# Attention into a mixture of experts on one core: order of the first loads, and products of ones in the first softmax

## The chip, the cores and the metric

The kernel runs on one core of a Trainium2 chip. The time is the device time of one execution in microseconds (us); three executions of the kernel before are shown, and their median is compared with that of the changed kernel. The profile comes from one further execution of its own. The engines are TensorE (PE, with its weight loads PEld), VectorE (DVE), ScalarE (ACT), GpSimd (POOL) and SyncE (SP), which here only issues transfers.

## The reference

There are four batches of q, k and v with 5056 rows of 256 channels, and eight experts with 1024 hidden units. A batch's attention is over channels, so its matrix is only 256 by 256, but it is a sum over all rows:

```
qn = q / (norm(q, axis=1) + 1e-6);  kn = k / (norm(k, axis=1) + 1e-6)
a  = softmax(kn.T @ qn / tau)              # 256 x 256 for each batch
x  = (v @ a).reshape(20224, 256)           # one row for each token
expert = argmax(x @ w_gate);  g = softmax(x @ w_gate)[expert]
out    = g * (relu(x @ w1[expert]) @ w2[expert])
```

## The kernel before

Each batch has two passes. The first reads q and k in 20 chunks (L205), adds up the products kn.T @ qn on PE (L225, or L229 and L230 where a chunk is split in two parts) and the squares of the entries on ACT and DVE (L215 to L218). Then comes the softmax (L242 to L327): the sums of squares go through PE into the PSUM tile `ntp`, DVE works out the reciprocal norms, two products with a diagonal (L272) spread those of q over the other half of `ntp`, DVE copies that half out (L287) and scales (L292), ACT takes the exponential (L299), PE transposes (L310), DVE copies (L314), PE multiplies by the gate's weights (L318), and DVE puts the result beside the attention matrix as `a_x` (L322). The second pass goes over v in ten groups of 512 tokens, each in two half groups (two `yield`s): first half, load v, `px` on PE (L365), copies and squares on ACT (L370, L372); second half, scale (L378), 16-bit rows on ACT and DVE (L386, L387), the choice of the expert and each row's place on DVE and PE (L395 to L442), and four scatters into the DRAM table `xs` from POOL's queue (L445).

The experts' weights are loaded and split into two 16-bit parts on the chip, by the generator `weights()`: 32 loads of 512 KB (L120), four for an expert, and for each matrix 16 products on PE for a scale (`gram`, L158), a diagonal (`w_diag`, L162), a product (L123), the scale (L84, L85), and a split of 128x2048 entries on ACT (L112) and then DVE (L113). One step of it issues one load; the splits of an expert's two matrices come with the first and the third load of the expert behind it. The second matrices of the last two experts are loaded into the tag `hl`, of two buffers, which also holds the squares of the next batch's chunks (L213, L217).

Once the six first groups of batch 0 are in `xs`, `table(0)` gives the list of full blocks of 256 tokens, and `block()` loads one transposed (L586), copies its expert's weights (L604) and multiplies (L616, L638). From there on, blocks and the passes of the batches that follow are interleaved by the pacing at L741 to L755.

The order of the work around the change is that of the Python program: its instructions are taken in this order for each engine, and where one isn't ready by the framework's planning, a later one can go ahead. All loads are in SP's queue. The main loop takes one half group of batch 0, some steps of the weights, and one chunk of batch 1, in turn. Step 20 (`step == nch`) is the first softmax; steps 21 and 22 are the first group's halves, and so on up to the sixth group:

```python
weighed = 0
for step in range(2, nch + 1 + 2 * CUT):
    take(first, 1)
    weighed += take(wts, 0 if step < nch else min(14 if step == nch else 2, 4 * E + 1 - weighed))
    if step > nch + 2:
        take(second, 1)
```

In the texts the experts' weights are counted in the order of loading (the first, the second, ...), and the splits too.

Of the kernel before, what the change touches and what calls it, by code (L numbers as in the profile page):

```python
# [10 lines left out]
F32 = mybir.dt.float32  # L11
# [9 lines left out]
P = 128  # L21
B, N, C = 4, 5056, 256
NP = 5120
E, F = 8, 1024
# [39 lines left out]
def attention_then_experts(ctx, tc, qk, vT, wts_in, kc, out):  # L64
    nc = tc.nc
    sync, act, vec, pool, pe = nc.sync, nc.scalar, nc.vector, nc.gpsimd, nc.tensor
# [6 lines left out]
    ps_h = ctx.enter_context(tc.tile_pool(name="ps_h", bufs=3, space=bass.MemoryType.PSUM))  # L73
# [111 lines left out]
    def split(raw):  # L185
# [3 lines left out]
        vec.tensor_tensor(out=hl[:, 1], in0=raw, in1=hl[:, 0], op=ALU.subtract)  # L189
        return hl  # L190

    def attention(b, s_split, x_split, acc):


# [4 lines left out]
        nch = len(s_split)  # L199
        behind = []  # L200
        for ch in range(nch):

            tag, bufs = (("raw", RAW), ("rows", 3), ("xg", 2), ("raw", RAW), ("rows", 3))[ch % 5 if b == 0 else 0]
# [39 lines left out]
        tp = ps_t.tile([P, 512], F32, tag="tp", name="ntp")  # L243
# [25 lines left out]
        for c in range(2):  # L269
            dg = soft[:, 0, c * P : (c + 1) * P]  # L270
            vec.tensor_scalar(out=dg, in0=ident, scalar1=rn[:, c : c + 1], scalar2=None, op0=ALU.mult)
            pe.matmul(tp[:, C + c * P : C + (c + 1) * P], ones, dg, start=True, stop=True)  # L272
        rq = tp[:, C : 2 * C]


        if x_split:
# [30 lines left out]
        tp = ps_t.tile([P, 512], F32, tag="tp", name="atp")  # L307
        for c1 in range(2):
            for c2 in range(2):
                pe.transpose(  # L310
                    tp[:, c2 * C + c1 * P : c2 * C + (c1 + 1) * P], a_x[:, c1, c2 * P : (c2 + 1) * P], ident
                )
        aT = soft[:, 5:7, :]
        vec.tensor_copy(out=aT, in_=tp.rearrange("p (c n) -> p c n", c=2))  # L314
        tp = ps_t.tile([P, 512], F32, tag="tp", name="gtp")
        for c1 in range(2):
            for c2 in range(2):
                pe.matmul(  # L318
                    tp[:, c1 * E : (c1 + 1) * E], aT[:, c2, c1 * P : (c1 + 1) * P], wg[:, c2, :],
                    start=(c2 == 0), stop=(c2 == 1),  # L320
# [21 lines left out]
        for g in range(G):  # L342
# [12 lines left out]
            for t in range(T):  # L355
                if b > 0:
                    px = ps_a.tile([P, C + E], F32, tag="acc", name="px")
                else:
                    pool_, tag = ((ps_y, "y0"), (ps_h, "hp"), (ps_y, "y1"), (ps_h, "hp"))[t]
                    px = pool_.tile([P, C + E], F32, tag=tag, name="px")  # L360
                ts = slice(t * P, (t + 1) * P)
                n = 0
# [58 lines left out]
            tp = ps_t.tile([P, 512], F32, tag="tp", name="rtp")  # L421
# [3 lines left out]
            for t in range(shifts):  # L425
                pe.matmul(
                    tp[:, t * E : T * E], ones16, ex[:, 0 : T - t, :].rearrange("p t e -> p (t e)"),
                    start=False, stop=(t == shifts - 1),
# [14 lines left out]
            for t in range(T):  # L443
                n = 64 if last and t == T - 1 else P
# [220 lines left out]
    def take(gen, n):  # L665
        for _ in range(n):
            next(gen, None)
        return n

    nch = NP // P // 2  # L670
    normal = [(ps_a, "acc")] * 2
    wts = weights()
    first = attention(0, [False] * nch, False, [(ps_y, "y0"), (ps_y, "y1")])
    second = attention(1, [i == 0 or i >= NATIVE for i in range(nch)], True, normal)

    ones16 = one.tile([P, P], F16, name="ones16")
    vec.memset(ones16, 1.0)
    idle = ps_t.tile([P, 512], F32, tag="tp", name="idle")
    for _ in range(30):
        pe.matmul(idle[:, 0:P], ones16, ones16, start=True, stop=True)  # L680
    take(first, 2)


# [22 lines left out]
    weighed = 0  # L706
    for step in range(2, nch + 1 + 2 * CUT):
        take(first, 1)
        weighed += take(wts, 0 if step < nch else min(14 if step == nch else 2, 4 * E + 1 - weighed))
        if step > nch + 2:  # L710
            take(second, 1)
    tables = {0: table(0)}

    def streams():
        tables[1] = table(1)
        for b in range(1, B):
            yield from second if b == 1 else attention(b, [True] * nch, True, normal)
            tables[b + 1] = table(b + 1)
            if b == B - 1:
                tables[LAST] = table(LAST)  # L720
            yield 0
# [76 lines left out]
```

## Time and profile before

| | us |
|---|---|
| median of 3 executions | 1184.86 (1183.29 to 1185.75) |
| the profiled execution | 1188.32 |
| its span, first to last instruction | 1186.6 |
| PE busy | 1153.5 (97%) |
| DVE busy | 899.4 (76%) |
| ACT busy | 643.5 (54%) |
| POOL busy | 392.3 (33%) |

The profiled execution is 1.7 us longer than its span, which is what lies around the first and the last instruction. A timeline row is: start and length in us, engine, line, operation, out<-in, shape, count, and in brackets the engine's idle time before it and what ended it. Rows of equal instructions in a row are merged.

### The profile page before, as it was taken

The page shows a single profiled execution, that of the slowest core. Times are in us where ns is not written, and L with a number is a line of the kernel's source. Part 1 is how long each engine was busy: PE and PEld are TensorE (multiplying, and loading weights), DVE is VectorE, ACT ScalarE, POOL GpSimd, SP SyncE. Part 2 cuts the span into 40 slices and gives each one's busy share as a digit, 9 for nine tenths or more (in the row PEclk, how much of TensorE's full clock was granted, in tenths as well). Part 3 has the DMA queues.
Part 4 walks back from the last instruction along what each step waited for, and adds up shares of the span by engine and source line. Part 5 has one row for each costly group of instructions (what it writes and reads, how often), then busy time and mean ns, then how long its engine had stood idle before and what let it go on. Part 6 is the DMA issues. An engine that isn't in the chain of part 4 may idle for free.

```text
span 1186.6 us, 28182 instructions
## 1 busy us (share of the span) xinstructions
PE 1153.5 (97%) x10242; PEld 1024.9 (86%) x10242; DVE 899.4 (76%) x2384; ACT 643.5 (54%) x1362; POOL 392.3 (33%) x366
## 2 busy tenths in 40 slices
PE   9798899999999999999999999999999999999998
PEld 8677688899888889999888889999988888889897
DVE  6789988778887877777888777776875566656886
ACT  6399854877655536665565536666533223332232
POOL 0046761466511123544422212455421111112121
PEclk9989989999999999999999999999999999999999
DMA  9977765445555524444354434443242222111121
GB/s 340 408 277 254 208 177 134 135 122 145 139 145 120 130 81 101 118 115 119 97 152 127 131 91 93 131 95 82 70 109 50 50 55 55 46 51 38 40 52 35
DMA packets 147871, 145.93 MB, mean 123 GB/s; under 512 B 115980, under 2 KB 117393, under 8 KB 147728
## 3 DMA queue, kind: packets, MB, share of 16 engines
q1 hardware_dynamic: 132336, 102.48, 33.0%
q0 software_dynamic: 15392, 41.60, 9.8%
q8 instruction: 82, 1.34, 0.5%
q14 instruction: 61, 0.50, 0.1%
HBM read 80.03 MB, written 43.29 MB: 104 GB/s over the span
## 4 chain that ended last, share of the span: by engine, by line
PE 57%; issue 24%; DVE 7%; POOL 5%; ACT 3%; DMA 3%; SPq 1%; POOLq 0%; DVEq 0%; ACTq 0%
PE y L638 20%; PE hp L616 19%; PE px L368 7%; POOL out L653 4%; PE sp L225 4%; PE sp L229 3%; DMA raw<-in_qk 2%; PE sp L230 2%; DVE W L113 1%; ACT xjunk L372 1%; PE px L365 1%; DVE rows L387 1%; DVE hl L189 1%; ACT W L112 1%; ACT xg L370 1%
## 5 line engine op out<-in xcount | busy, mean ns | idle before, releaser
L616 PE MATMUL hp<-xT,wp 128*128 128x256 f16 (+1 forms) x4320 | 450.0, 262 | 1.6 <-DVE ht L624 1.1
L638 PE MATMUL y<-wp,ht 128*128 128x256 f16 x3888 | 447.7, 273 | 0.0
L616 PEld LDWEIGHTS <-wp 128*128 128x128 f16 x4320 | 383.1, 98 | 46.1 <-issue 3.4
L638 PEld LDWEIGHTS <-ht 128*128 128x128 f16 x3888 | 373.9, 98 | 53.3 <-issue 4.7
L653 POOL DMA_INDIRECT out<-o,mt x162 | 184.9, 1141 | 628.5 <-ACT o L651 595.2
L604 DVE COPY wp<-W 128x1024 f16 x720 | 297.8, 425 | 116.0 <-PE y L638 65.3
L623 ACT ACTIVATE ht<-hp 128x512 f16<-128x512 f32 x324 | 191.6, 593 | 157.1 <-PE hp L616 143.1
L624 DVE SCALAR_TENSOR_TENSOR ht<-hp,ht 128x512 f16<-128x512 f32 x324 | 219.6, 686 | 22.6 <-ACT ht L623 16.6
L445 POOL DMA_INDIRECT xs<-rows,r_si x160 | 189.5, 1184 | 122.7 <-issue 41.8
L651 ACT ACTIVATE o<-y,b_fac 128x256 f32<-128x256 f32 x162 | 68.8, 470 | 207.2 <-PE y L638 196.6
L368 PE MATMUL px<-a_h,hl 128*128 128x264 f32 x480 | 98.1, 296 | 0.0
L386 ACT ACTIVATE rows<-xg,x_sc 128x256 f16<-128x256 f32 x160 | 69.9, 497 | 25.7 <-DVE r_ex L419 16.0
L368 PEld LDWEIGHTS px<-a_h,hl 128*128 128x128 f32 x480 | 78.8, 188 | 1.6 <-issue 0.6
L189 DVE TENSOR_TENSOR hl<-raw,hl 128x1024 fp32r<-128x1024 f32 x47 | 57.4, 1221 | 26.7 <-ACT hl L188 26.7
L188 ACT CAST hl<-raw 128x1024 fp32r<-128x1024 f32 x47 | 49.1, 1044 | 45.2 <-PE sp L230 38.2
L229 PE MATMUL sp<-hl 128*128 128x512 f32 x188 | 72.3, 418 | 1.1 <-DVE hl L189 1.1
L225 PE MATMUL sp<-raw 128*128 128x256 f32 x264 | 65.3, 403 | 7.5 <-DMA raw<-in_qk 7.5
L387 DVE SCALAR_TENSOR_TENSOR rows<-xg,x_sc,rows 128x256 f16<-128x256 f32 x160 | 69.5, 477 | 1.2 <-ACT rows L386 0.8
L217 ACT ACTIVATE raw<-raw 128x1024 f32<-128x1024 f32 x44 | 46.6, 1058 | 42.6 <-DVE hl L189 42.4
L372 ACT ACTIVATE xjunk<-xg 128x256 bf16<-128x256 f32 x160 | 66.7, 417 | 3.2
L368 PE MATMUL px<-a_l,hl 128*128 128x264 f32 x240 | 68.2, 284 | 0.0
L225 PEld LDWEIGHTS sp<-raw 128*128 128x128 f32 x264 | 52.0, 202 | 15.9 <-DMA raw<-in_qk 8.6
(144 smaller groups left out, 926.4 us busy)
## 6 DMA issues: line engine op xcount, KB each, us to landing
raw<-in_qk SPq DMA_DIRECT2D x80, 512.0 KB, 4.2
vraw<-in_vT SPq DMA_DIRECT2D x34, 512.0 KB, 5.1
W<-in_w SPq DMA_DIRECT2D x28, 512.0 KB, 8.5
v<-in_vT SPq DMA_DIRECT2D x12, 256.0 KB
out<-o,mt POOLq DMA_INDIRECT x162, 2.4
xs<-rows,r_si POOLq DMA_INDIRECT x160, 4.0
wraw<-in_w SPq DMA_DIRECT2D x4, 512.0 KB, 6.5
xT<-xs SPq DMA_TRANSPOSE x90, 3.9
```

The costliest lines, as they stand in the source:

```text
L225: pe.matmul(sp[c][:, 0, :], raw[:, j, kc0 : kc0 + P], raw[:, j, 0:C], start=first, stop=last)
L229: pe.matmul(sp[c], hl[:, 0, j, kc0 : kc0 + P], hl[:, :, j, 0:C], start=first, stop=False)
L368: pe.matmul(px, hl[:, vh, c, ts], ah[:, c, :], start=(n == 0), stop=(n == 5))
L372: act.activation(junk, xg[:, t, 0:C], AF.Square, accum_out=ss[:, t : t + 1])
L387: vec.scalar_tensor_tensor(out=r16[:, t, C : 2 * C], in0=x, scalar=sc[:, t : t + 1], in1=r16[:, t, 0:C], op0=ALU.mult, op1=ALU.subtract,)
L445: ins = pool.indirect_dma_start(out=xs[:, :], out_offset=bass.IndirectOffsetOnAxis(ap=si[:n, t : t + 1], axis=0), in_=rows[:n, t, :], in_o ...
L604: copied[0] = vec.tensor_copy(out=t, in_=Wf[:, ds(e * 8192 + n * 1024, 1024)]).ins
L616: pe.matmul(hp[:, f % nf, :], wp[:, dc, wh, (f % 2) * P : (f % 2 + 1) * P], xT[:, 2 * xh + dc, :], start=(n == 0), stop=(n == 5),)
L623: act.activation(ht[:, 0], hp, AF.Relu)
L624: vec.scalar_tensor_tensor(out=ht[:, 1], in0=hp, scalar=0.0, in1=ht[:, 0], op0=ALU.max, op1=ALU.subtract)
L638: pe.matmul(ys[j], hts[f // nf][:, hh, f % nf, j * P : (j + 1) * P], wp[:, f % 2, wh, :], start=(f == 0 and n == 0), stop=(f == 7 and n == 2),
L653: pool.indirect_dma_start(out=out[:, :], out_offset=bass.IndirectOffsetOnAxis(ap=mt.bitcast(I32)[:, j, 1:2], axis=0), in_=o, in_offset=Non ...
```

## The change

Three edits. A helper `busy(bank, n)` makes n products of a 128x128 tile of ones by itself into the first 128 columns of a PSUM tile; nothing reads them. Batch 0's softmax calls it twice: 24 products into `ntp`, behind L272 and ahead of L287, and ten into a tile of its own from the tag `hp`, behind the transposes of L310 and ahead of L314. Of the weights, ten loads (the first two experts and one matrix of the third) stand ahead of the first group's v, where it was 14, then two in each of the two halves of the first group, as before, and then three in each half group, where it was two, until all are out.

```diff
+    def busy(bank, n):
+
+        for _ in range(n):
+            pe.matmul(bank[:, 0:P], ones16, ones16, start=True, stop=True)
...
         rq = tp[:, C : 2 * C]
+        if b == 0:
+            busy(tp, 24)
...
+        if b == 0:
+            none = ps_h.tile([P, 512], F32, tag="hp", name="none")
+            busy(none, 10)
         aT = soft[:, 5:7, :]
...
-    for _ in range(30):
-        pe.matmul(idle[:, 0:P], ones16, ones16, start=True, stop=True)
+    busy(idle, 30)
...
-        weighed += take(wts, 0 if step < nch else min(14 if step == nch else 2, 4 * E + 1 - weighed))
+        weighed += take(wts, 0 if step < nch else min(10 if step == nch else 2 if step < nch + 3 else 3, 4 * E + 1 - weighed))
```

## Rows read from the trace of the kernel before

**Rows 1.** The page, its first part: busy time, share of the span and instructions of each engine.

```profile
PE 1153.5 (97%) x10242; PEld 1024.9 (86%) x10242; DVE 899.4 (76%) x2384; ACT 643.5 (54%) x1362; POOL 392.3 (33%) x366
```

**Rows 2.** Busy time by stretch: from:to, length, busy us (and instructions) of PE, PEld, DVE, ACT and POOL, then PE's granted clock, the DMA engines' share and GB/s.

```profile
50.00:60.00 10.00, 4.36 (x43) 3.69 (x41) 7.34 (x17) 6.25 (x4) 0.00 (x0) 0.78 1.04 403
60.00:120.00 60.00, 51.78 (x362) 43.31 (x360) 55.94 (x139) 57.31 (x122) 35.51 (x23) 0.95 0.74 264
...
200.00:400.00 200.00, 197.70 (x1697) 176.47 (x1695) 164.53 (x449) 134.88 (x297) 79.36 (x76) 1.00 0.50 134
400.00:1186.00 786.00, 778.94 (x7355) 698.75 (x7352) 569.76 (x1507) 369.01 (x802) 232.63 (x229) 1.00 0.33 85
```

**Rows 3.** The chain of waits that ended last, in order of time: start, length, engine and line.

```profile
48.48 2.35 DVE W L113
...
58.63 3.74 PE px L365 x8
...
112.11 2.36 DVE W L113
...
115.58 4.37 DMA raw<-in_qk
...
130.68 5.07 DMA xs<-rows,r_si
135.90 1.34 SPq L586
...
143.04 5.36 DMA raw<-in_qk
148.44 3.78 PE sp L225 x8
```

**Rows 4.** PE's timeline.

```profile
1.06 3.38 PE L680 MATMUL idle<-ones 128*128 128x128 f16 x30 [1.06 <-DVE ones L677]
...
51.38 0.38 PE L123 MATMUL gram<-w_dsum,ones 128*128 128x2 f32 x2 [0.77 <-DVE w_diag L162]
51.63 1.53 PE L158 MATMUL gram<-W 128*128 128x128 bf16 x24
58.04 0.59 PE L123 MATMUL gram<-w_dsum,ones 128*128 128x2 f32 x2 [4.88 <-DVE w_diag L162]
58.49 5.70 PE L365 MATMUL px<-a_x,v 128*128 128x264 f32 x16
...
67.60 2.47 PE L365 MATMUL px<-a_x,v 128*128 128x264 f32 x10
...
88.04 1.89 PE L225 MATMUL sp<-raw 128*128 128x256 f32 x8
```

**Rows 5.** DVE's timeline.

```profile
42.95 0.42 DVE L287 COPY soft<-ntp 128x256 f32<-128x256 f32 x1 [0.61 <-PE ntp L272]
...
47.88 0.69 DVE L314 COPY soft<-atp 128x512 f32<-128x512 f32 x1 [0.55 <-PE atp L310]
...
50.74 0.17 DVE L322 COPY a_x<-gtp 128x16 f32<-128x16 f32 x1
...
58.66 0.16 DVE L84 TENSOR_SCALAR pw_m<-gram 128x2 int32<-128x2 int32 x1 [0.68 <-PE gram L123]
...
59.69 4.61 DVE L113 SCALAR_TENSOR_TENSOR W<-W,scales 128x2048 f16<-128x2048 f32 x2 [0.66 <-ACT W L112]
64.83 0.19 DVE L395 TENSOR_REDUCE r_m<-xg 128x4 f32<-128x32 f32 x1 [0.53 <-ACT xg L370]
...
120.57 2.32 DVE L113 SCALAR_TENSOR_TENSOR W<-W,scales 128x2048 f16<-128x2048 f32 x1
122.81 1.22 DVE L218 TENSOR_TENSOR ssq<-ssq,sq 128x1024 f32<-128x1024 f32 x1
...
124.16 0.19 DVE L442 TENSOR_REDUCE r_si<-r_sl 128x4 int32<-128x32 f32 x1
```

**Rows 6.** ACT's timeline.

```profile
50.91 3.90 ACT L112 ACTIVATE W<-W,scales 128x2048 f16<-128x2048 f32 x2 [2.74 <-DVE W L113]
57.65 3.90 ACT L112 ACTIVATE W<-W,scales 128x2048 f16<-128x2048 f32 x2 [2.84 <-issue]
61.51 0.38 ACT L370 COPY xg<-px 128x264 f32<-128x264 f32 x1
62.39 0.38 ACT L370 COPY xg<-px 128x264 f32<-128x264 f32 x1 [0.50 <-PE px L365]
```

**Rows 7.** SP's timeline: the loads of the weights ahead of the first v, and the first v.

```profile
26.48 13.71 SPq L120 DMA_DIRECT2D W<-in_w  x14
41.14 5.69 SPq L340 DMA_DIRECT2D v<-in_vT  x4
```

**Rows 8.** PE alone by stretches of 2 us: from:to, length, PE busy, granted clock, DMA share, GB/s.

```profile
46.00:48.00 2.00, 1.00 (x14) 1.00 1.04 416
...
56.00:58.00 2.00, 0.00 (x0) 0.50 1.03 395
```

**Rows 9.** POOL's timeline: scatters of the fourth, fifth and sixth group.

```profile
112.68 2.63 POOL L445 DMA_INDIRECT xs<-rows,r_si  x1 [0.30 <-ACT xjunk L372]
...
121.06 3.80 POOL L445 DMA_INDIRECT xs<-rows,r_si  x1 [0.30 <-issue]
125.22 0.96 POOL L445 DMA_INDIRECT xs<-rows,r_si  x1 [0.36 <-ACT W L112]
```

## The prediction

> **What bounds the kernel now.** I read the page's busy shares first: PE is busy for 97% of the span [rows 1], so the time is PE's work plus what PE loses. The busy time by stretch says where it loses: from 200 us on it is busy 197.7 of 200 and 778.9 of 786 us at the full clock, while from 50 to 60 us it works only 4.36 of 10, at a mean clock of 0.78, and from 60 to 120 us 51.8 of 60 [rows 2]. The change touches the first 120 us alone, and behind it nothing is left to win, so I take it that a shift of the point where the blocks start passes to the end one for one. What sets that point is read from the chain of waits, and then from each engine's timeline along it.
>
> The chain goes through the split of weights on DVE at 48.48, through the first group's px at 58.63, later through a split at 112.11 and a load of q and k at 115.58 that lands 4.37 us later, through the sixth group's scatter, which lands at 135.75, to the first block's transposed load at 135.90; behind three such loads in SP's queue a chunk is issued only at 143.04, and PE gets it at 148.44 [rows 3]. So the sixth group's scatter is the gate. Between 60 and 120 us ACT is busy 57.3 and DVE 55.9 of 60 us [rows 2]: both are nearly full, and the chain there is work, not waiting. ACT has its two avoidable pauses just ahead: 2.84 us before 57.65 and 0.50 us before 62.39 [rows 6].
>
> **The change part by part.** *Ten loads instead of 14 ahead of v.* SP needed 13.71 us for 14 loads, 0.98 each, so v is issued some 3.9 us earlier than at 41.14 [rows 7]. By itself this is worth nothing, because `a_x` was ready only at 50.91 (50.74 + 0.17) [rows 5] and px did not start until 58.49 [rows 4]. What held PE for the 4.88 us before 58.04 was the third expert's scale product L123, waiting for `w_diag`, which stood on DVE behind two splits [rows 4]. With ten loads that product, its diagonal and two of the five splits stand behind the first group's px. Then PE can go on when the second expert's scale product ends, 51.38 + 0.38 = 51.8 [rows 4], and what is late next is ACT: it still does the second and the third split from 50.91 to 54.81 [rows 6], and takes the first copy of px right there instead of at 61.51 [rows 6]. The fourth and fifth split, 3.90 us, move behind the group's copies, so ACT wins not 6.7 us but its pauses: 2.84 + 0.50 = 3.3 us. The pause of 2.74 us before 50.91 stays, since that split waits for DVE's first one. On DVE, the pauses of 0.68, 0.66 and 0.53 us at 58.66, 59.69 and 64.83 [rows 5] go, 1.9 us, less a new one, since the group's small operations would now wait for ACT's copies. Ends: 0 if DVE is the limit and its new pause eats the old ones; 6.7 us (58.49 less 51.8) if the first group's lead were kept whole. I take ACT's 3.3, since ACT is the fuller of the two in the stretch behind [rows 2].
>
> PE's clock is a gain that hides: after the 4.88 us pause the granted clock is 0.50 (1.2 GHz) [rows 8], and eight products of px take 3.74 us [rows 3] against 10 in 2.47 us at 2.4 GHz [rows 4]: 8 x (0.468 - 0.247) = 1.8 us. ACT is at its splits meanwhile; in the sum 0.
>
> *24 products into ntp.* In the kernel before, 24 products of this size took 1.53 us at the full clock [rows 4], and 30 took 3.38 us at 1.2 GHz, 113 ns each [rows 4]. They stand in PE's queue behind L272; behind them wait the products for the first expert's scale, and so the first split on ACT. They write columns 0 to 127 of `ntp`, and DVE's L287 reads columns 256 to 511. If L287 waits for them as it waited for L272 until 42.95 [rows 5], the whole softmax, one serial line from there to `a_x`, is late by them; the last of them drains while DVE starts, so 1.4 us of the 1.53. If it waits only for the products that write what it reads, 0. At 1.2 GHz it would be 24 x 0.113 = 2.7 us. I take 1.4: each reader of a PSUM tile in these rows starts after the last product into that tile ahead of it, and the granted clock from 46 to 48 is 1.00 though PE works only half of it [rows 8]. That row also says that the clock there has nothing to win from the products.
> The Trainium skill ("PSUM — Partial Sum Buffer", section "PSUM bank collisions raise a hardware error") says that a TensorE write and a VectorE read must not meet in one bank, at disjoint columns too, and that software has to guard by bank; no row here shows such a pair. By that page the wait of 1.4 us is certain; without it the sum below would be 1.4 us lower, 1180.7.
>
> *Ten products into none.* 10/24 of 1.53 us, 0.6 us, between the transposes and the gate's product. They lie beside L314 (0.69 us at 47.88), and the result of the gate's product waits on DVE behind a split until 50.74 anyway [rows 5]: 0. Were L322 taken ahead of that split, they would cost at most 0.6. Nothing else queues for long: the bank they take from `hp` is one of three, and the first expert's is free by then.
>
> *Three loads a half group.* The count of loads issued is behind by four at step 20, level at step 26 (26 of 32) and ahead by one, then two, then one from step 27 to 29. No byte is added; the total of 26 loads ahead of batch 1's fourth chunk is the same, so the stretch with full DMA ends as before, and the 16 splits cost the same 2.35 us of DVE each [rows 3]. But the last four come earlier against the fifth and sixth group. There POOL is held up while DVE splits: scatters that begin under a split last 2.63 and 3.80 us, where the one at 125.22 takes 0.96 [rows 9]. Two splits fewer beside the last groups free POOL of 2 x (2.63 - 0.96) = 3.4 us, yet the sixth group's places were ready on DVE only at 124.35 and POOL took them at 125.22 [rows 5, 9]: with DVE's order unchanged at most 0.9 us is to be had. Ends 0 and 3.4; I take 0.9.
>
> Sum: +1.4 - 3.3 - 0.9 = -2.8 us. Against the profiled execution that is 1188.3 - 2.8 = 1185.5 us; it stands 3.5 us above the median of the three runs, and outside them, so the forecast for a median is 1184.86 - 2.8 = 1182.1.
>
> **The rivals.** *Nothing to be seen: DVE is the limit.* For it: DVE is busy 55.9 of 60 us, and its avoidable pauses of 1.9 us less a new one of some 0.5 just pay for the 1.4 us of products. Against it: ACT is fuller. The same comes out if the planning leaves the third expert's scale ahead of px. Time: 1184.9.
>
> *A larger gain.* After the sixth group's counts DVE did a split of 2.32 us and a sum of 1.22 us, 120.57 to 123.94, before its places [rows 5]. If the earlier weights let that split go by before, or the places go first, 3.5 us more fall out of the chain: 1182.1 - 3.5 = 1178.6. For it: the seventh and eighth experts' loads move up. Against: on a full DVE a split done earlier delays the groups in between.
>
> *Slower: both hl buffers taken too early.* The last expert's second matrix now asks for its `hl` buffer one chunk earlier, ahead of batch 1's sixth chunk. Until the split of the one before it is done, both buffers hold weights, no square can be made, raw buffers stay taken, and SP's queue, with v behind, stands still. Before, this cost PE a wait for the load of 115.58, 4.37 us long [rows 3], off the gate's path, and a cold start, where eight products take 3.78 [rows 3] instead of 1.89 us [rows 4]. It decides once a chunk or a v stands so late in SP's queue that the fifth or sixth group's px waits for it: then 4.4 + 1.9 = 6.3 us more, less the 2.8: +3.5, 1188.4. Against: by then loads are ahead and DVE has work in store.
>
> **How the numbers follow.** A measurement of this kernel can tell about 0.2%, 2.4 us, from no change. Forecast 0.37 (1182.1, its own spread 1180.5 to 1183.8, so 0.22 faster and 0.15 the same); no change 0.28 (0.22 the same, 0.03 on either side); larger gain 0.17; slower 0.18. Faster 0.42, same 0.37, slower 0.21. Both large cases hold too much to be cut off whole: the range takes in most of either, 1177.5 to 1188.5.
>
> **What would show it.** Right: no pause of PE above 2 us between 50 and 60 us, a granted clock of 1.00 at the first px, px from about 53 us, ACT's first copy of px near 56, no pause of ACT above 1 us between 52 and 60. L287 near 44.3 instead of 42.95 would show the products' price, L287 at 42.95 that there is none. The sixth group's last scatter should land near 133 instead of 135.75, and the first transposed load with it. Wrong: an early px with the sixth group's scatter no earlier (DVE was the limit), or a wait for raw longer than 4.37 us before the first block (the buffers).

## The result, and the profile after

The changed kernel took 1192.01 us (median of five executions, 1190.64 to 1193.86), the kernel before beside it 1185.61 us: a ratio of 1.0052, with an interval of 1.0032 to 1.0072. Forecast were 1182.1 us, within 1177.5 to 1188.5. It is slower by some 6 us where 2.8 us were to be won. The lines of the changed kernel are those of before up to L190, then five, then seven, and from L314 on ten higher (px is L375, the last write of the table L581).

PE's busy share is the same as in [rows 1]:

```profile
PE 1158.7 (97%) x10276; PEld 1029.0 (86%) x10276; DVE 898.4 (75%) x2384; ACT 643.1 (54%) x1362; POOL 382.9 (32%) x366
```

By stretch, as in [rows 2] (busy us of PE, PEld, DVE, ACT, POOL, then PE's granted clock):

```profile
50.00:60.00 10.00, 9.12 (x28) 7.41 (x28) 7.71 (x11) 5.84 (x9) 0.00 (x0) 0.53 1.03 406
60.00:120.00 60.00, 50.05 (x370) 41.23 (x369) 51.23 (x127) 51.66 (x106) 30.87 (x22) 0.94 0.69 248
```

From 50 to 60 us PE is busy twice as long as before, and it is no gain: it runs there at 1.2 GHz, and ACT works less than before (5.84 us against 6.25). From 60 to 120 us DVE does 4.7 us less of its work (55.94 before) and ACT 5.7 us less (57.31). That is where the loss arises: not in longer work, since DVE's total is the same, but in work not done in time. By the view of waits ACT waits 5.5 us for px between 60 and 120 us, before 1.1, and PE twice waits some 3 us for DVE: for the difference of a chunk (L189), and for the diagonal of a scale product, which comes behind a split on DVE (93.81 to 96.15). Before, the same waits were 1.15 and at most 0.96 us:

```profile
78.80 0.50 PE L234 MATMUL sp<-hl 128*128 128x512 f32 x1 [3.15 <-DVE hl L189]
...
96.76 0.38 PE L123 MATMUL gram<-w_dsum,ones 128*128 128x2 f32 x2 [3.00 <-DVE w_diag L162]
```

PE's timeline, as in [rows 4], and PE alone by 2 us (PE busy, granted clock), as in [rows 8]:

```profile
8.20 0.61 PE L195 MATMUL none<-ones 128*128 128x128 f16 x8
...
40.67 0.27 PE L195 MATMUL none<-ones 128*128 128x128 f16 x2
...
53.27 6.86 PE L375 MATMUL px<-a_x,v 128*128 128x264 f32 x16
```

```profile
48.00:50.00 2.00, 1.35 (x12) 0.81 1.04 414
50.00:52.00 2.00, 1.94 (x9) 0.50 1.01 398
```

The px is early (53.27 instead of 58.49), but the clock fell to 1.2 GHz about 49 us, some 6 us earlier than before, though the kernel before had less for PE to do ahead of it (0.82 of the 2 us from 44 to 46, here all 2.00). This can't be put down to the change: with the order of before held and nothing changed, the clock fell at about 47 us in the profile (last section). And the ten products aren't in the second gap: they wait for nothing, so the planning put eight at 8.20 and two at 40.67.

ACT's timeline, as in [rows 6]: the copies come at 56.30, as forecast, but each of the next waits for a px at half the clock, 1.92 us in all, where 3.34 us of pauses were to go.

```profile
56.30 0.38 ACT L380 COPY xg<-px 128x264 f32<-128x264 f32 x1
57.18 0.38 ACT L380 COPY xg<-px 128x264 f32<-128x264 f32 x1 [0.50 <-PE px L375]
...
58.94 0.38 ACT L380 COPY xg<-px 128x264 f32<-128x264 f32 x1 [0.97 <-PE px L375]
...
60.17 0.38 ACT L380 COPY xg<-px 128x264 f32<-128x264 f32 x1 [0.45 <-PE px L375]
```

DVE's timeline, as in [rows 5], from the copy out of `ntp` to the first table (from `c_ni` to the last write of `c_tb`):

```profile
44.39 0.42 DVE L294 COPY soft<-ntp 128x256 f32<-128x256 f32 x1 [1.95 <-PE ntp L195]
...
60.58 0.19 DVE L405 TENSOR_REDUCE r_m<-xg 128x4 f32<-128x32 f32 x1 [1.58 <-ACT xg L380]
61.53 0.17 DVE L388 TENSOR_SCALAR x_sc<-x_ss 128x4 int32<-128x4 int32 x1 [0.76 <-ACT xjunk L382]
...
129.91 0.15 DVE L517 SCALAR_TENSOR_TENSOR c_ni<-ctp,kt 1x8 int32<-1x8 f32 x1
...
133.71 2.35 DVE L113 SCALAR_TENSOR_TENSOR W<-wraw,scales,W 128x2048 f16<-128x2048 f32 x1 [2.57 <-ACT W L112]
...
140.58 0.18 DVE L581 TENSOR_SCALAR c_tb<-c_sf 1x5 int32<-1x5 f32 x1
```

The copy is 1.44 us late (42.95 before), as the products' price was put. At the end stands what the prediction didn't look at: the table. Its last write is at 140.76, and in the middle of it DVE waits 2.57 us for ACT's half of a split, does its own half and a sum of squares. Before, a split lay in the table as well, but the table began at 125.24, and its last write was over at 133.88, 2 us ahead of the gate:

```profile
125.24 0.15 DVE L507 SCALAR_TENSOR_TENSOR c_ni<-ctp,kt 1x8 int32<-1x8 f32 x1 [0.90 <-PE ctp L505]
...
133.73 0.15 DVE L571 TENSOR_SCALAR c_tb<-c_sf 1x5 int32<-1x5 f32 x1
```

POOL's and SP's timelines (the sixth group's last scatter, the first and the seventh transposed load; before 130.68, 135.90 and 201.37):

```profile
132.51 0.96 POOL L455 DMA_INDIRECT xs<-rows,r_si  x1 [0.30 <-issue]
```

```profile
141.67 1.33 SPq L596 DMA_TRANSPOSE xT<-xs  x1
...
204.90 1.25 SPq L596 DMA_TRANSPOSE xT<-xs  x1
```

The scatter is 1.8 us late, the first load 5.8, because it now waits for the table: it starts 0.91 us behind the last write, and 0.92 behind it with the loads alone and with the products alone, below. By the seventh load 2.2 us of that are given back; the 3.5 us left there stay to the end (the span is 3.6 us longer). So the difference is settled at some 200 us, and the seventh load tells more of it than the first: in the profiles of these two kernels and of the first eleven runs below, what lies behind that load is always 985.1 to 985.7 us long. This pair of profiles shows only 3.6 of the 6.4 us between the medians, since the profiled execution of the kernel before was 2.7 us above its median.

### The profile page after: what moved, and what is told of

The parts are those of the page before. It is cut to its first block, busy times and chain, and to the rows that moved or that the text cites. A ratio compares the mean times of both kernels' runs of the same rounds, so it can differ in the third digit from the quotient of the medians.

```text
span 1190.2 us, 28244 instructions
## 1 busy us (share of the span) xinstructions
PE 1158.7 (97%) x10276; PEld 1029.0 (86%) x10276; DVE 898.4 (75%) x2384; ACT 643.1 (54%) x1362; POOL 382.9 (32%) x366
## 5 line engine op out<-in xcount | busy, mean ns | idle before, releaser
L663 POOL DMA_INDIRECT out<-o,mt x162 | 182.2, 1125 | 629.6 <-ACT o L661 596.4
L455 POOL DMA_INDIRECT xs<-rows,r_si x160 | 180.4, 1128 | 131.8 <-issue 43.8
L378 PE MATMUL px<-a_h,hl 128*128 128x264 f32 x480 | 98.2, 296 | 0.0
L378 PEld LDWEIGHTS px<-a_h,hl 128*128 128x128 f32 x480 | 78.8, 188 | 1.6 <-issue 0.6
L189 DVE TENSOR_TENSOR hl<-raw,hl 128x1024 fp32r<-128x1024 f32 x47 | 57.4, 1222 | 25.5 <-ACT hl L188 25.2
L397 DVE SCALAR_TENSOR_TENSOR rows<-xg,x_sc,rows 128x256 f16<-128x256 f32 x160 | 69.5, 478 | 4.0 <-ACT rows L396 3.6
L380 ACT COPY xg<-px 128x264 f32<-128x264 f32 x160 | 57.9, 367 | 21.5 <-PE px L375 11.1
L378 PE MATMUL px<-a_l,hl 128*128 128x264 f32 x240 | 68.0, 284 | 0.0
```

The lines of the kernel that those rows point to most:

```text
L378: pe.matmul(px, hl[:, vh, c, ts], ah[:, c, :], start=(n == 0), stop=(n == 5))
L397: vec.scalar_tensor_tensor(out=r16[:, t, C : 2 * C], in0=x, scalar=sc[:, t : t + 1], in1=r16[:, t, 0:C], op0=ALU.mult, op1=ALU.subtract,)
L455: ins = pool.indirect_dma_start(out=xs[:, :], out_offset=bass.IndirectOffsetOnAxis(ap=si[:n, t : t + 1], axis=0), in_=rows[:n, t, :], in_o ...
L663: pool.indirect_dma_start(out=out[:, :], out_offset=bass.IndirectOffsetOnAxis(ap=mt.bitcast(I32)[:, j, 1:2], axis=0), in_=o, in_offset=Non ...
```

## The experiments

Every ratio is of 5 to 12 executions against the kernel before, run beside them on the same chip, with its 95% interval; the ratio of the medians can differ from it by some 0.001. Four runs went first at the parts, with the order planned anew for each.

**The loads alone**, without products:

```diff
-        weighed += take(wts, 0 if step < nch else min(14 if step == nch else 2, 4 * E + 1 - weighed))
+        weighed += take(wts, 0 if step < nch else min(10 if step == nch else 2 if step < nch + 3 else 3, 4 * E + 1 - weighed))
```

> The new order of loads (10, then 2, then 3), without any of the products of ones. If the products are the cost (theory A: 1.4 us on the softmax's line and what follows from it), this is no slower than before: ratio 0.997 to 1.001, DVE's copy of ntp back at 42.95. If the order of the weights is the cost (theory B: splits and scale products now stand ahead of groups and of the table in DVE's and PE's queues), it is as slow as the whole change: ratio 1.004 to 1.007, and PE again waits some 3 us for a w_diag between 90 and 100 us.

Measured: 1.0024 (1.0008 to 1.0041). The first transposed load was at 139.92, behind a table ending at 139.0; px ran at 52.93 with the clock at 0.50 from about 47 to 57 us, without any product of ones. The ratio lies between the two theories: the copy is back (43.01), but the time isn't, and the wait of 3 us for a w_diag doesn't come either (PE's longest from 90 to 100 us is 0.40).

**The products alone**, 24 and ten, loads as before:

```diff
+        if b == 0:
+            busy(tp, 24)
...
+            none = ps_h.tile([P, 512], F32, tag="hp", name="none")
+            busy(none, 10)
```

> The products of ones (24 and 10), with the loads as before (14, then 2). Theory A: ratio 1.004 or more. Theory B: only the 1.4 us that DVE's copy of ntp is late, ratio 1.000 to 1.0015, and the first transposed load within 2 us of 135.90.

Measured: 1.0047 (1.0032 to 1.0062), 5.6 us, four times the 1.44 us of the late copy, with the table's end at 140.6. That is theory A by the time; the run with the order held, below, shows that it isn't the own cost of the 24.

**Ten loads, then two**, no products:

```diff
-min(14 if step == nch else 2, 4 * E + 1 - weighed)
+min(10 if step == nch else 2, 4 * E + 1 - weighed)
```

> Ten loads ahead of the first group and then two in each half group, no products: the loads' first half of the edit alone. If the three loads a half group are what hurts in theory B, this is no slower than before, 0.997 to 1.001; if it is the first group's place itself, 1.004 or more.

Measured: 1.0068 (1.0046 to 1.0091). By its forecast the first group's place would be what costs, and it is the dearest of the parts; but with the order held, below, that place alone costs 0.0012.

**The whole change with the products pinned**: the 24 in a bank of their own behind the second L272, the ten behind the transposes.

```diff
-            busy(tp, 24)
+            gap = ps_h.tile([P, 512], F32, tag="hp", name="gap")
+            with tc.issue_after(spread.ins):
+                busy(gap, 24)
...
-            busy(none, 10)
+            with tc.issue_after(turned.ins):
+                busy(none, 10)
```

> The whole change, but the 24 products go to a PSUM bank of their own behind L272's products, and the ten are held behind the transposes, where the planning had moved them to the start of the kernel. DVE's copy of ntp should be back near 42.95 under every theory. Theory A: ratio at most 1.001, and if the cold clock from 49 us on comes from the ten products missing, the granted clock stays 1.00 from 46 to 54 us. Theory B: 1.003 or more, with the late table as in the changed kernel.

Measured: 1.0064 (1.0039 to 1.0088), though DVE's copy was now at 42.61, not late at all. So a loss of that size comes without the wait at the shared bank too. The ten products, now in their gap (47.67), didn't keep the clock up: it was 0.53 from 46 to 48 us and 0.50 on to 56. And it is a new order again, with px only from 57.01, so the run doesn't price the wait by itself.

All four are slower, and by more than the work that they add. The instruction lists of the programs show why that can be: of DVE's first 420 instructions 134 stand elsewhere in the changed kernel than before, with the loads alone 150, with the products alone 135. It needs no product on DVE: 24 products on PE move 80, one moves none. The planning takes each instruction when it thinks it ready, and a small delay at 42 us turns its choices over all the way to 140 us. So the next runs **held the order**: each engine's instructions chained, by dependencies that only order, in the sequence of one of the two kernels.

**The 24 products, all else in the order of before:**

```diff
+            busy(tp, 24)
...
+    hold(ORDER_OF_BEFORE)
```

> The kernel before, with the 24 products of the first softmax behind the second spread product, and every engine held to the instruction order of before (the ten products are left out). Theory A, the products themselves cost the time (their writes into the bank from which DVE copies, and the clock): the ratio stays near that of the products with their own planned order, 1.0047; 1.003 or more. Theory B, the loss lies in the order that the planning gives the engines once anything ahead of it has changed: what is left is the 1.44 us by which the copy of ntp came later, so a ratio of 0.9990 to 1.0015, the copy near 44.4 us and the first xT near 136 to 137.5 us.

Measured: 1.0009 (0.9998 to 1.0021), outside the interval of the products planned anew (where the ten were in too). In its profile the copy is where the products put it, 1.18 us late:

```profile
44.13 0.42 DVE L342 COPY soft<-ntp 128x256 f32<-128x256 f32 x1 [1.95 <-PE ntp L240]
```

For the time theory B holds. Its forecast of the first transposed load missed (139.62 instead of 136 to 137.5): that execution was 3 us above the median of its kernel.

**The changed kernel in its own order, without the 24 products:**

```diff
-            busy(tp, 24)
...
+    hold(ORDER_OF_AFTER)
```

> The changed kernel with the order of every engine held to its own, and only the 24 products taken out (the ten stay). Theory A: the time falls by the products' share, to a ratio of about 1.001 or less against before. Theory B: it stays at the changed kernel's 1.0052 less at most 1.44 us, 1.0038 to 1.0055, with the table's last write near 139 to 141 us.

Measured: 1.0039 (1.0027 to 1.0051). Three quarters of the loss stay without them. With the run before, that shows that the order makes most of it: the planned order as a whole, with the places of the moved loads, which are part of it, and with the ten products at 8.20 and 40.67. The clock doesn't: its mean over an execution, which the record has for each, is 0.991 here against 0.990 in the kernel before beside it, and 0.990 in both with the products alone.

**The first group in front by hand**, the order of before but for three moves (lines of the kernel before):

```diff
 PE
-L123 (third expert), L365 x8
+L365 x8, L123
 ACT
-L112 x2, L370 and L372 x8
+L370 and L372 x8, L112 x2
 DVE
-L113 x2, L395 L397 L378 L400 L402 L406
+L395 L397 L378 L400 L402 L406, L113 x2
```

> The kernel before, held to its own order on every engine but for three moves by hand: PE's eight px products of the first group ahead of the ones-product of the third expert's first pair, ACT's four copies and four squares of px ahead of that pair's two splits, and DVE's first six instructions on the logits ahead of its two splits. No products of ones, loads as before. If the prediction's step was right (ACT fills its pause of 2.84 us and its queue runs that much earlier): px near 53.5 us, no pause of ACT over 1 us from 52 to 60, first xT near 133 us, ratio 0.9970 to 0.9985. If the front is bound by DVE's work, or gives the time back before the first stage: 0.9990 to 1.0010. If the first group in front is harmful by itself (its rows or its clock): 1.002 or more.

Measured: 1.0012 (1.0001 to 1.0023), between the second and the third forecast, with the first transposed load at 137.20: the prediction's mechanism, alone, gives nothing. The lines of the held runs are 45 or more higher than before. PE, ACT and DVE:

```profile
54.31 4.26 PE L410 MATMUL px<-a_x,v 128*128 128x264 f32 x16
...
66.91 0.58 PE L168 MATMUL gram<-w_dsum,ones 128*128 128x2 f32 x2 [4.77 <-DVE w_diag L207]
```

```profile
56.38 0.82 ACT L415 COPY xg<-px 128x264 f32<-128x264 f32 x2 [1.39 <-PE px L410]
...
59.67 3.88 ACT L157 ACTIVATE W<-W,scales 128x2048 f16<-128x2048 f32 x2
66.34 2.00 ACT L157 ACTIVATE W<-W,scales 128x2048 f16<-128x2048 f32 x1 [2.79 <-DVE W L158]
```

```profile
61.70 4.61 DVE L158 SCALAR_TENSOR_TENSOR W<-W,scales 128x2048 f16<-128x2048 f32 x2 [1.19 <-ACT W L157]
...
68.38 2.35 DVE L158 SCALAR_TENSOR_TENSOR W<-W,scales 128x2048 f16<-128x2048 f32 x1 [1.52 <-ACT W L157]
```

ACT's pause of 2.84 us before 57.65 [rows 6] is down to 1.39. But the two splits that were moved behind the copies start 2.0 us later on DVE (59.69 before [rows 5]). The next scale product stands behind them on PE and waits 4.77 us, the 4.88 us of before once more, with the second group's px behind it; and ACT has a pause of 2.79. The stall was moved one pair of splits on, not removed.

**The changed kernel with the first table in one piece on DVE:**

```diff
 DVE, order of after
-c_p x4, L113, L223, c_p x2, ..., L581
+c_p x6, ..., L581, L113, L223, ...
```

> The changed kernel, held to its own order on every engine, but DVE's 19 instructions of the first table in one piece: the split, the sum of squares and the seven instructions on rows that stood among them come behind the table. Theory gate: the first stage waits for the table alone, so c_tb near 134 us and the first xT near 136 to 137 us instead of 141.67, and of the 6.4 us lost some 4 to 5 come back: ratio 1.0005 to 1.0025. Theory lag: DVE and ACT are 6 us behind in all of their front work, and what is moved behind the table is paid in the first stage: 1.004 or more, though xT comes earlier.

Measured: 1.0029 (1.0009 to 1.0049), by the ratios 2.7 us of 6.2 back, by the medians 4.1 of 6.4 (three of the twelve executions took 1195 to 1198 us), between the two theories. The two intervals overlap, but the profile shows the step (DVE, then SP's first and seventh transposed load):

```profile
129.81 0.15 DVE L568 SCALAR_TENSOR_TENSOR c_ni<-ctp,kt 1x8 int32<-1x8 f32 x1
...
133.54 0.16 DVE L632 TENSOR_SCALAR c_tb<-c_sf 1x5 int32<-1x5 f32 x1
133.66 2.35 DVE L161 SCALAR_TENSOR_TENSOR W<-wraw,scales,W 128x2048 f16<-128x2048 f32 x1
```

```profile
139.34 1.33 SPq L647 DMA_TRANSPOSE xT<-xs  x1
...
202.66 1.25 SPq L647 DMA_TRANSPOSE xT<-xs  x1
```

From `c_ni` to the last write it takes 3.9 us instead of 10.8. The table starts as late as in the changed kernel, 4.6 us later than before, and the first load gains only 2.3 us, for now the scatters come last: POOL's next step waited for one until 139.36. That remainder is the lag of the front, which this edit doesn't touch.

**The two groups in front by hand**: the moves of the first group, and the same for the second.

```diff
 PE
-L123, L365 x5
+L365 x5, L123
 ACT
-L112, L386 x4, L410, L370 and L372 x8
+L386 x4, L410, L370 and L372 x8, L112
 DVE
-L113, L387 x4, ..., L395 to L416
+L387 x4, ..., L395 to L416, L113
```

> The kernel before in its own order, with the first group in front as in the three moves by hand (DVE now seven instructions on the logits), and the same done for the second group: PE's last five px products of it ahead of the next ones-product, ACT's rows of the first group and the copies and squares of the second ahead of the next split, DVE's rows of the first group and its logits of the second ahead of its half of that split. Theory, the stall was only moved one pair on (ACT 2.79 and DVE 1.52 and 1.19 us in the run before this): those go, the px of the second group ends before 66 us, DVE's busy time from 50 to 80 us is 1.5 to 2.5 us above the 23.56 us of that run, and the ratio is 0.9980 to 0.9995. Rival, DVE's total of work sets the front from 60 us on and any filled pause is paid back there: 1.0000 to 1.0015, with the first xT at 136 to 138 us. Rival, holding DVE's splits back costs more: over 1.002.

Measured: 0.9983 (0.9968 to 0.9999). The stalls behind the first group's px are gone or short (ACT's timeline; then busy time from 50 to 80 us in the kernel before, the run with one group, and this one):

```profile
55.05 0.82 ACT L415 COPY xg<-px 128x264 f32<-128x264 f32 x2 [0.56 <-PE px L410]
...
62.13 1.69 ACT L431 ACTIVATE rows<-xg,x_sc 128x256 f16<-128x256 f32 x4
...
66.69 3.88 ACT L157 ACTIVATE W<-W,scales 128x2048 f16<-128x2048 f32 x2
```

```profile
50.00:80.00 30.00, 22.24 (x173) 18.65 (x171) 25.65 (x60) 25.51 (x47) 6.35 (x4) 0.88 0.85 333
```

```profile
50.00:80.00 30.00, 22.84 (x168) 19.00 (x165) 23.56 (x57) 23.99 (x43) 5.24 (x4) 0.83 0.86 335
```

```profile
50.00:80.00 30.00, 23.84 (x177) 19.96 (x175) 27.23 (x65) 28.19 (x55) 9.46 (x5) 0.90 0.88 332
```

One group in front costs DVE 2.1 us of work done by 80 us, two win 1.6 us over the kernel before, and ACT 2.7. Yet the first transposed load is at 135.85, as before. SP's timelines show where the lead goes, not by what (this run, then the kernel before):

```profile
104.22 0.80 SPq L165 DMA_DIRECT2D wraw<-in_w  x2
114.89 0.33 SPq L250 DMA_DIRECT2D raw<-in_qk  x1
...
135.85 1.34 SPq L631 DMA_TRANSPOSE xT<-xs  x1
...
199.62 1.27 SPq L631 DMA_TRANSPOSE xT<-xs  x1
```

```profile
106.64 0.80 SPq L120 DMA_DIRECT2D wraw<-in_w  x2
115.58 0.33 SPq L205 DMA_DIRECT2D raw<-in_qk  x1
...
201.37 1.26 SPq L586 DMA_TRANSPOSE xT<-xs  x1
```

2.4 us ahead at `wraw`, 0.7 at `raw`, nothing at the first block; 1.75 us ahead again at the seventh load; which work that is wasn't traced.

**Three loads alone**, behind the fourteen, planned anew:

```diff
-min(14 if step == nch else 2, 4 * E + 1 - weighed)
+min(14 if step == nch else 2 if step < nch + 3 else 3, 4 * E + 1 - weighed)
```

> Three loads in the later half groups behind the fourteen of before, no group moved in front, no products; the order is planned anew. If three loads by themselves give the 0.44% by which ten and three stood below ten and two: ratio 0.995 to 0.997. If the difference between those two was a matter of the order that each happened to get: anything from 0.999 to 1.005, with the table or the sixth group's scatter at the gate by that order.

Measured: 1.0011 (1.0001 to 1.0022). Three loads give nothing of their own; that speaks for the order that each got as the reason why ten and three stood below ten and two.

**The table in one piece and no 24 products** (both edits above, in the order of after):

> The changed kernel in its own order with DVE's first table in one piece and without the 24 products. If the parts add up (products 0.0013, the table cut on DVE 0.0023 of the 0.0052): 1.0010 to 1.0025. If the products are free once the table is whole (the sixth group's rows then come last): 1.0025 to 1.0035.

Measured: 1.0029 (1.0013 to 1.0045), the same as with the products. The parts don't add up to a tenth of a per cent; this run can't say whether the products are free there.

**The order of before held, and nothing changed:**

> The kernel before with the order of its instructions on every engine held by ordering-only dependencies, and nothing else changed. If holding an order is neutral, as the readings of the held runs assume: ratio 0.9990 to 1.0010. If it costs or gives something by itself: outside of that, and the other held runs have to be read against this one.

Measured: 0.9991 (0.9973 to 1.0008). Holding is neutral to within some 0.2%, so the held runs can be read against the kernel before.

In this run and all that follow the kernel before takes 1222 to 1223 us: what lies behind the seventh transposed load is 1014 to 1021 us long in all seven profiles, 28 to 36 us longer than in those up to here. There, **the third stall** (the two groups, and at 110 us PE's eight L158 behind the next two px products and DVE's two L162 behind L378, L395, L397):

> The two groups in front by hand, and in addition at 110 us: PE's eight products of a split half that waited 2.08 us for the load of wraw come behind the two px products that ACT waits for, and DVE's two w_diag behind its first three instructions on those logits. Theory, the lead of the two groups (2.4 us at the load of wraw, 0.7 at the next load of raw) is lost there, because ACT's 2.14 us pause for px delays the square that releases raw: the pause goes, the load of raw is issued near 113 instead of 114.89 us, and the ratio comes to 0.996 to 0.998. Rival, the front is held there by DVE's work: no better than the two groups alone, 0.998 to 1.000.

> The two groups in front and the third stall removed, once more, because the first time it ran on a chip on which the stages after 230 us take 35 us longer for every kernel, the one before among them, and no lead of the front reached the end there. Theory, the lead is lost at 110 us behind ACT's pause for px: 0.1 to 0.2% below the two groups alone. Rival, DVE's work holds the front there: within 0.1% of the two groups alone.

Measured: 0.9992 (0.9969 to 1.0015) and 1.0014 (0.9994 to 1.0033). **The two groups with the 24 products:**

> The two groups in front by hand with the 24 products of the first softmax behind the second spread product, the order of all else as in that run. If the products cost what the copy of ntp waits for and give nothing: 1.0 to 1.5 us above the two groups alone, a ratio of 0.999 to 1.0005. If they keep the clock up for the px of the first group: px's 16 products in under 3.0 us instead of 3.78, and a ratio of at most 0.9985.

> The two groups in front with the 24 products, once more for the same reason. If the products cost the 1.44 us for which the copy of ntp waits: 0.1% above the two groups alone, 0.0 to 0.2%. If they give by the clock more than that: at least 0.05% below it.

Measured: 0.9993 (0.9972 to 1.0013) and 1.0000 (0.9984 to 1.0016). **The two groups again:**

> The two groups in front by hand once more, as the base of the two runs beside it and on another chip than the first time. If the 0.17% by which it was below the kernel before are its own: 0.9968 to 0.9995. If they were chance at the edge of an interval: 0.9995 to 1.0015.

> The two groups in front by hand a third time, in the hope of a chip on which the kernel before takes its usual 1186 us: only there does a difference of the front reach the end. If the first result stands: 0.9965 to 0.9995 on such a chip. If it was chance: 0.9995 to 1.0015. On a chip where the kernel before takes some 1222 us it decides nothing.

Measured: 1.0000 (0.9980 to 1.0020) and 1.0014 (0.9991 to 1.0036). None of these six tells its theories apart. That the two groups beat the kernel before rests on one run at the edge of its interval and was not seen again. For the mechanism speaks the pair with one group and with two from the earlier time, 1.0012 (1.0001 to 1.0023) against 0.9983 (0.9968 to 0.9999); it isn't shown by it, for the run with two groups was on another chip and also had the higher mean clock (0.992, against 0.990 with one group and in the kernel before).

## Why the prediction was wrong

**"ACT wins its pauses: 2.84 + 0.50 = 3.3 us."** This is the step that failed. Nearly all that it named came: px at 53.27 (forecast 53), ACT's copy at 56.30 (56), no pause of PE above 2 us from 50 to 60, none of ACT above 1 us. But the two splits moved behind the copies were counted as moved for nothing, and the run with one group moved by hand shows the price: DVE's half of them starts 2.0 us later, and behind it the next scale product and the next group's px stall as long as the first had (4.77 against 4.88 us). In place of -3.3 us that run measured +1.4 us (0.0012 of 1187.5, with an interval from 0.1 to 2.7). With the second group moved too it came to -2.0 us, once. In the changed kernel, where the planning put the splits elsewhere, it isn't that one stall: there PE waits for DVE until 78.80 and until 96.76, and ACT for px 5.5 us in place of 1.1.

**"PE's clock ... in the sum 0."** The hidden gain didn't come. The granted clock at the first px was 0.50, not 1.00, and ACT waited for px 1.92 us in all. The 30 products at the start, which the prediction read as 1.2 GHz by their 113 ns, stand in the trace at a granted clock of 1.00; no term hung on it. DVE's new pause, put at some 0.5 us, was 1.58 + 0.76.

**"24 products into ntp: +1.4."** Right: the copy was 1.44 us late, and with the order held the kernel 0.0009, 1.1 us (an interval from -0.2 to 2.5). The row shows the wait at disjoint columns that the Trainium skill ("PSUM — Partial Sum Buffer", section "PSUM bank collisions raise a hardware error") asks software to keep; what would happen without it no run here shows.

**"Ten products into none ... 0."** The place was wrong (8.20 and 40.67, not the second gap). A price of their own wasn't measured: the products alone ran with both sets.

**"Three loads a half group: -0.9."** Wrong: alone 1.0011, and in the changed kernel the sixth group's scatter was 1.8 us later, not earlier: what it waits for came late (the sixth group's counts on DVE at 125.86, before at 120.35). Its upper end, 2 x (2.63 - 0.96), is 3.3 and not 3.4.

**"So the sixth group's scatter is the gate", and "a shift ... passes to the end one for one."** The gate went to the table, which no row of the prediction held, though it ended only 2 us ahead of the gate. The rival of the buffers, too, took the load of 115.58 for "off the gate's path", though the chain in [rows 3] goes through it. And the shift at the gate is not what arrives: 5.8 us late at the first transposed load became 3.5 at the seventh and 3.6 in the span.

**What was missing from the sum** is the planned order. The prediction wrote "with DVE's order unchanged"; 134 of DVE's first 420 instructions were moved, and the products fall from 1.0047 (all 34, planned anew) to 1.0009 (the 24, order held). Of the loss of 0.0052, 0.0039 is there without the 24 products; the table cut on DVE is by the ratios 0.0023 of the loss with the products and 0.0010 without. How the rest of the order's price divides stays open.

Of the rivals, "DVE is the limit" had the nearest mechanism (early px, no earlier scatter), but forecast no change. "Both hl buffers taken too early" had the sign and about half the size (1188.4), but not the place: the longest wait for raw was 2.42 us, not over 4.37. SP did stand still for a weight's buffer, longer than the 6.3 us of before; the view of waits on SP's queue (total, times, longest):

```profile
SPq L120 <- DVE ssq L223: 14.5, 2, 12.0
```

That the squares release it late is the lag of DVE; no run separated it from that lag.

## What to carry to other kernels

Where a planner sets the order, compare the instruction lists of both kernels before a term is put on any single edit, and hold the order to measure an edit by itself: 24 small products cost 0.09% so, and with ten more and the order planned anew 0.47%. When work is pulled ahead of a stalled step, follow what it pushes back to its next reader; a pause filled in one place came back at full length one pair later until that reader was moved too. And list every input of the gate with its slack, not only the one that came last.

## What was not expected of the hardware

The fall of PE's clock in the first softmax is not settled by the program. With the order of before it fell at about 55.5 us in the kernel before, in a pause of PE of 4.88 us, and at about 47.4 us in the later run with that order held and nothing changed, in a pause of 1.00 us. From 48 to 50 us (busy us of all engines, then PE's granted clock; the kernel before, then that run):

```profile
48.00:50.00 2.00, 1.67 (x23) 1.50 (x21) 2.00 (x2) 0.18 (x1) 0.00 (x0) 1.00 1.02 392
```

```profile
48.00:50.00 2.00, 2.00 (x15) 1.74 (x13) 1.27 (x2) 0.56 (x1) 0.00 (x0) 0.50 1.03 395
```

In the runs with one and with two groups in front PE's instructions up to 60 us are the same, yet the stretch from 48 to 50 us was at 1.00 in one profile and 0.85 in the other, and the 16 products of the first px took 4.26 and 3.78 us. With the same kernel in two of the later runs, the two groups with products, the mean clock from 50 to 60 us was 1.00 and 0.83, and the first transposed load came at 135.15 and 140.6 us. A single profile can thus lie some 5 us off another of the same kernel in the front, as much as the whole effect; ratios over many executions and a held order were needed to see it.

The kernel before took 1185 to 1188 us in the earlier runs and 1222 to 1223 us in the later ones, 3% more, and nearly all of it lies behind the seventh transposed load. That it is a matter of the chip isn't shown: the record gives chip 4 for runs of both kinds. Why was not studied.
